# Block-window attention into a mixture of experts on one core: first products of all pair passes from scaled float16 parts

## The chip, the cores and the metric

One core of a Trainium2 chip runs the whole program. The metric is the device time of one execution in microseconds; the kernel's time is the median over runs. TensorE (PE) multiplies, VectorE (DVE), ScalarE (ACT) and GpSimd (POOL) do elementwise work and move results out of PSUM, SyncE (SP) issues all DMA transfers, in order.

## The reference

```python
# q, k, v: [4, 8, 768, 64]; block = 32, window = 16
k_sum = k.reshape(B, H, 24, 32, D).max(axis=3)
v_sum = v.reshape(B, H, 24, 32, D).mean(axis=3)
a = softmax(concat([scale * q @ k.T masked to |i - j| < 16,
                    scale * q @ k_sum.T + log(32)]))
attn = a @ concat([v, v_sum])
x = attn.transpose(0, 2, 1, 3).reshape(3072, 512)
p = domain_probs / (domain_probs.sum(-1, keepdims=True) + 1e-9)
for e in range(4):                       # w1[e]: 512 x 1024, w2[e]: 1024 x 512
    out += p[:, e:e + 1] * (np.maximum(x @ w1[e], 0) @ w2[e])
```

Every token goes through all four experts; the output is float32.

## The kernel before, in words

The 3,072 tokens are eight blocks of 384 (`TB`), two to each batch entry b. A plan (line 1183) walks through six stages: block 0 with experts 0, 1; block 1 with experts 1, 0; blocks 0 and 1 together with experts 2, 3 (the plain stages, named [0], [1] and [0,1] here); then three pairs of blocks, pair 1 (blocks 2, 3) with experts 3, 2, 1, 0, pair 2 with 0 to 3 and pair 3 with 0 to 3. The attention that makes the x of a later pair runs in between, in steps that have each a due time on the scale of the plan (`steps`, `advance`); pair 1's x is made in the plain stages, pair 2's in pair 1, pair 3's in pair 2. Nothing of it is left for pair 3. The order within each engine is then made by a scheduler from the program order and priorities, so that rows of an engine can stand otherwise than in the code.

Precision comes from parts: a matrix is split into a high and a low part, and a product is three matmuls, high x high, high x low, low x high. The plain stages use float32 parts (`ph` tiles, `plain_units`): per expert and hidden chunk of 128, twelve matmuls of 384 columns; ACT makes the high part `hh` of the relu, and DVE the low part `hl` (`to_h`), which frees the PSUM bank. The second product (`po` tiles, 128x512) sums over the chunks.

The pair stages (`pair_units`) use a scheme with seven instead of eight products for the two blocks and two halves of the weights (`SEVEN`): for each of four index pairs i, seven combinations of w1 (`WS`) times seven combinations of x (`XS`), six matmuls of 128x384 each (two chunks by three part products), in PSUM tiles pha, phb, phc, phd. The combinations of x are made by `x_operands` from raw x that was written to DRAM (`xs`, `xraw`) as attention left PSUM.

Pairs 1 and 2 have float32 parts. `w1_operands` makes the seven combinations of w1 with their parts in pair 1 (ACT copies, DVE and POOL subtractions), and stores each of the seven (256 KB) in DRAM; pair 2 loads them again, seven loads a set. Pair 3 (`SCALED`) has float16 parts in both products. For that the weights and v are scaled by powers of two found from their largest magnitudes: in pair 2, DVE scans the w1 combinations (`scan_w1`, 16 rows of 256 columns for each expert) and w2 (`scan_w2`, 8 rows of 512 columns); v's maximum is found for b = 3 alone (`setup_v_part`). `spread_maxima` writes the maximum of each partition to DRAM and loads all 128 to every partition; `take_maxima` reduces them and makes a scale and its inverse. `prepare` loads raw w1 and w2 again and makes the scaled float16 combinations of w1 (`ws`, `wss`) and parts of w2 (`w2s`) at listed points of pair 2's last expert and of pair 3 (`LATE`, `FIRST`, `SECOND`); raw x is scaled by DVE in `x_operands`. `mixed` folds the inverse scales into the mixing weights `pw` (a copy `pm`).

`with_fetch` fetches the next expert's weight sets at units 1 and 8 of a second product. In SBUF a pool tag "w1" has NW1 = 14 tiles, of which a float32 set takes 7, and a tag "x" has NX tiles, of which the x of a pair takes 14 in float32 and 7 in float16.

Everything goes through a recording helper, so nearly all instructions show line 79 in the profile; they are told apart by the names of their tiles. The names: `aw` are the attention weights, `awT` their transposes (by DMA), `px` the attention output in PSUM, `psc` the scores, `ms`, `rs`, `nb` softmax tiles, `vch` a chunk of v, `vsr` its block sums, `found` the columns of maxima and scales, `xr` raw x of a pair, `x_t`, `xl_t`, `xh_t` combinations of x.

Of the kernel before, what the change touches and what calls it, by code (L numbers as in the profile page):

```python
# [66 lines left out]
def attn_moe(ctx: ExitStack, tc: tile.TileContext, qvL, qv0, v0L, kD, kT, vT, w1L, w2L, dpL, cst, out):  # L67
# [69 lines left out]
    pending, last_matmul = [], [None]  # L137

    def spread_maxima():

        for t in pending:
            m, k, name = t["m"], t["k"], t["name"]
            room = dram.tile([P, k], F32, name=f"{name}d")
            SP.dma_start(room, m)
            t["every"] = every = sb.tile([P, P, k], F32, name=f"{name}e", tag="hs", bufs=2)
            flat = room.rearrange("p k -> (p k)").rearrange("(o n) -> o n", o=1)
            SP.dma_start(every.rearrange("p q k -> p (q k)"), flat.broadcast_to([P, P * k]))

    def take_maxima():
        while pending and "every" in pending[0]:  # L150
            t = pending.pop(0)
            ins = V.tensor_reduce(t["m"], t["every"].rearrange("p q k -> p k q"), axis=AX.X, op=ALU.max)
            behind(ins, last_matmul[0])
            t["then"](*scales(t["m"], t["k"]))

    def scales(m, k):

        both = facts(2 * k)
        s, inv = both[:, 0:k], both[:, k : 2 * k]
# [72 lines left out]

    def setup_v(b):
        for hp in range(H // 2):
            if b < SCALED or hp == H // 2 - 1:
                setup_v_part(b, hp)
        vsr, top = vstats[b]
        stack_v(b, vsr)
        if b == SCALED:
            m = facts(1)  # L240
            V.tensor_reduce(m, top, axis=AX.X, op=ALU.max)
            pending.append(dict(m=m, k=1, name="v", then=lambda *s: v_scale.update({b: s})))
# [164 lines left out]
    def to_x(n):  # L407
# [15 lines left out]
        A.mul(xs[:, 0], pair[0], 1.0 / ASC)  # L423
        A.mul(xs[:, 1], pair[1], 1.0 / ASC)
# [9 lines left out]
    def x_operands(pr):  # L434
        if pr == SCALED:
            xp = {}
            for w in XS:
                both = sb.tile([P, 2, 2, TB], F16, name=f"x{pr}_{w}", tag="x", bufs=NX)
                xp[w] = both[:, 0], both[:, 1]
        else:  # L440
            xp = {w: [x_half(f"x{v}{pr}_{w}") for v in "hl"] for w in XS}
# [341 lines left out]
    def w1_operands(e, pr):  # L783
        ws = {w: w1_part(f"w1{w}{e}_{pr}") for w in WS}
        if (e, pr) in stored:
            for w in WS:
                SP.dma_start(ws[w].bitcast(F32), stored[e, pr][w])
# [13 lines left out]
        parts("11", a11, PL)  # L801
        parts("22", a22, V)
# [3 lines left out]
        parts("s2", a11, V)  # L806
        parts("s1", a22, PL)
        parts("s3", a21, V)
        parts("12", a12, PL)
# [12 lines left out]
    KINDS = ("11", "12", "22", "s3")  # L822

    def scan_w1(ws, i, m):

        if m in SCANS:
            w = SCANS[m]
            largest(top1[:, KINDS.index(w), i : i + 1], ws[w][:, 0:256].bitcast(F32))

    SCANS = {0: "11", 1: "s3", 2: "12", 3: "22"}  # L830

    def scan_w2(fc, w):
        largest(top2[:, fc : fc + 1], w[0].bitcast(F32))

    def maxima_of(e):

        V.tensor_reduce(kinds, top1, axis=AX.X, op=ALU.max)
        V.tensor_tensor(kinds[:, 0:1], kinds[:, 0:1], kinds[:, 3:4], op=ALU.add)
        V.tensor_reduce(most[:, 0:1], kinds[:, 0:3], axis=AX.X, op=ALU.max)
        V.tensor_reduce(most[:, 1:2], top2, axis=AX.X, op=ALU.max)  # L840

        def then(s, inv):
            V.tensor_scalar_mul(s[:, 1:2], s[:, 1:2], W2TOP)
            V.tensor_scalar_mul(inv[:, 1:2], inv[:, 1:2], 1.0 / W2TOP)
            w_scale[e] = s, inv

        pending.append(dict(m=most, k=2, name=f"w{e}", then=then))
# [3 lines left out]
    def prepare():  # L851

        jobs = [
            (which, e, i)
            for e in PAIRS[-1][1]
            for which, i in ((0, 0), (0, 1), (1, 0), (1, 1), (0, 2), (0, 3), (1, 2), (1, 3))
        ]
# [2 lines left out]
        def load(which, e, i):  # L860
            raws[which, e, i] = [load_weights((w1L, w2L)[which], e, 2 * i + j, "12"[which] + "s") for j in range(2)]

        def parts(t, raw, s):
            behind(A.activation(t[:, 0], raw, AF.Copy, scale=s), last_matmul[0])
            V.scalar_tensor_tensor(t[:, 1], raw, s, t[:, 0], op0=ALU.mult, op1=ALU.subtract)
# [3 lines left out]
        for (which, e, i), after in zip(jobs, jobs[1:] + [None]):  # L869
            s = w_scale[e][0][:, which : which + 1]  # L870
            r1, r2 = raws.pop((which, e, i))
            if after:
# [1 line left out]
            if which == 1:
                w = sb.tile([P, 2, 2, 512], F16, name=f"w2s{e}_{i}", tag="w2", bufs=FC)
                for j, r in enumerate((r1, r2)):
                    parts(w[:, j], r, s)
                    half2[e, 2 * i + j] = w[:, j, 0], w[:, j, 1]
                    yield
                continue  # L880
            a11, a12 = r1[:, 0:256], r1[:, 256:512]
            a21, a22 = r2[:, 0:256], r2[:, 256:512]
            ws = ready[SCALED, e, i] = {}

            def group(names, raw):
                t = sb.tile([P, 2, 256 * len(names)], F16, name=f"ws{names[0]}{e}_{i}", tag="w1", bufs=NW1)
                parts(t, raw, s)
                for o, w in enumerate(names):
                    ws[w] = tuple(t[:, v, 256 * o : 256 * (o + 1)] for v in range(2))

            group(("11", "12"), r1)
            group(("22",), a22)
            PL.tensor_tensor(a22, a21, a22, op=ALU.add)
            PL.tensor_tensor(a21, a11, a21, op=ALU.subtract)
            yield
            group(("s3", "s1"), r2)
            PL.tensor_tensor(a11, a22, a11, op=ALU.subtract)
            PL.tensor_tensor(a12, a12, a11, op=ALU.subtract)
            yield
            group(("s2", "s4"), r1)  # L900
            yield
# [2 lines left out]
    FIRST, SECOND = (0, 2, 4, 7, 9, 11, 14, 16, 18, 20), (1, 2, 4, 5, 7, 8, 10, 11, 13, 14)
    LATE = (0, 1, 2, 4, 5, 7, 8, 13, 14, 15, 16)

    mix = {}

    def mixed(e):

# [363 lines left out]
```

## Time and profile before

| | us |
|---|---|
| median of 3 runs | 1165.96 (1163.51 to 1166.89) |
| profiled execution, time | 1165.11 |
| profiled execution, span | 1163.3 |
| PE busy | 1136.3 (98%) |
| DVE / ACT / POOL busy | 747.8 / 597.8 / 521.3 |

| stage | from, to (us) |
|---|---|
| [1], expert 1 | 132.4 to 174.8 |
| [1], expert 0 | 174.8 to 214.2 |
| [0,1], expert 2 | 214.2 to 290.8 |
| [0,1], expert 3 | 290.8 to 375.0 |
| pair 1 | 375.0 to 653.4 |
| pair 2 | 653.4 to 924.4 |
| pair 3 | 924.4 to 1163 |

The profile is of one execution. A row of a group gives engine, operation, output and input tile, shape, count, then the busy time and the mean duration in ns of one, then the idle time before such instructions and what ended it. A row of the chain gives start, duration, engine, tile and how many instructions in a run. A row of the waits reads: who waited, for whom, total us, times, longest. A row of the windows gives the stretch, its length, and the busy time (and count) of each engine, then the granted clock of PE as a share of full speed, the DMA share and GB/s.

### The profile page before, as it was taken

The page shows a single profiled execution, that of the slowest core. Times are in us where ns is not written, and L with a number is a line of the kernel's source. Part 1 is how long each engine was busy: PE and PEld are TensorE (multiplying, and loading weights), DVE is VectorE, ACT ScalarE, POOL GpSimd, SP SyncE. Part 2 cuts the span into 40 slices and gives each one's busy share as a digit, 9 for nine tenths or more (in the row PEclk, how much of TensorE's full clock was granted, in tenths as well). Part 3 has the DMA queues.
Part 4 walks back from the last instruction along what each step waited for, and adds up shares of the span by engine and source line. Part 5 has one row for each costly group of instructions (what it writes and reads, how often), then busy time and mean ns, then how long its engine had stood idle before and what let it go on. Part 6 is the DMA issues. An engine that isn't in the chain of part 4 may idle for free.

```text
span 1163.3 us, 21120 instructions
## 1 busy us (share of the span) xinstructions
PE 1136.3 (98%) x7212; PEld 921.4 (79%) x7212; DVE 747.8 (64%) x1783; ACT 597.8 (51%) x1682; POOL 521.3 (45%) x642
## 2 busy tenths in 40 slices
PE   9898899999989999999999999999999999999998
PEld 7888789998977989889898998989888754545454
DVE  5679776554797745658677665747557874646461
ACT  5578567665565746447365433525334453535350
POOL 2398687846695746548266212212102222222220
PEclk9999999999998999999999999999999999999999
DMA  6699787966986877879994677849581532222211
GB/s 241 204 286 323 232 234 238 272 176 175 328 241 177 271 229 257 253 242 301 304 269 126 193 208 206 285 124 334 136 250 54 140 98 73 74 73 73 73 37 55
DMA packets 195564, 228.78 MB, mean 197 GB/s; under 512 B 82560, under 2 KB 119296, under 8 KB 195456
## 3 DMA queue, kind: packets, MB, share of 16 engines
q1 hardware_dynamic: 195456, 227.43, 65.5%
q8 instruction: 57, 0.93, 0.3%
q14 instruction: 51, 0.42, 0.1%
HBM read 153.32 MB, written 57.15 MB: 181 GB/s over the span
## 4 chain that ended last, share of the span: by engine, by line
PE 75%; DMA 8%; DVE 6%; POOL 4%; ACT 3%; issue 2%; SPq 1%; POOLq 0%; ACTq 0%; DVEq 0%
PE po L79 38%; PE phb L79 12%; PE pha L79 7%; PE phc L79 4%; PE phd L79 4%; PE psc L79 3%; PE ph L79 3%; PE px L79 2%; DMA wr<-in_w2L 2%; DMA vch<-in_vT 1%; DMA wr<-in_w1L 1%; PE pav L79 1%; DMA awT<-aw 1%; DVE xr L79 1%; POOL wl L79 1%
## 5 line engine op out<-in xcount | busy, mean ns | idle before, releaser
L79 PE MATMUL po<-w,hh 128*128 128x512 f32 x1152 | 361.6, 395 | 0.0
L79 PEld LDWEIGHTS po<-w,hh 128*128 128x128 f32 x1152 | 212.7, 189 | 45.4
L79 PE MATMUL po<-w,hl 128*128 128x512 f32 x576 | 227.4, 397 | 0.0
L79 POOL TENSOR_TENSOR ks<-kr,ks 128x304 fp32r<-128x304 f32 x112 | 100.0, 899 | 184.7 <-ACT ks L79 176.3
L79 PEld LDWEIGHTS po<-w,hl 128*128 128x128 f32 x576 | 108.4, 188 | 23.8
L79 DVE CUSTOM_DVE_ANT_0 ms<-psc,c_sb 96x152 f32<-96x152 f32 x256 | 68.9, 306 | 80.0 <-PE psc L79 76.1
L79 PE MATMUL po<-w2s,hh 128*128 128x512 f16 (+1 forms) x400 | 114.2, 370 | 0.0
L79 ACT ACTIVATE ms<-ms,nb 96x152 f32<-96x152 f32 x256 | 104.3, 416 | 17.2 <-DVE nb L79 16.6
L79 DVE TENSOR_TENSOR aw<-ms,aw 96x512 f16<-96x512 f32 x112 | 77.9, 728 | 29.0 <-ACT aw L79 28.6
L79 POOL TENSOR_TENSOR wr1s<-wr1s 128x256 f32<-128x256 f32 x32 | 27.8, 870 | 151.3 <-DVE ws L79 136.7
L79 PE MATMUL ph<-xh,wh 128*128 128x384 f32 x256 | 88.1, 348 | 4.5 <-ACT wh L79 3.7
L79 ACT CAST ks<-kr 128x304 fp32r<-128x304 f32 x112 | 48.2, 445 | 82.6 <-PE psc L79 65.5
L79 PE MATMUL ph<-xl,wh 128*128 128x384 f32 x256 | 87.2, 341 | 2.3 <-DVE xl L79 2.3
L79 PE MATMUL ph<-xh,wl 128*128 128x384 f32 x256 | 87.4, 343 | 1.6 <-POOL wl L79 1.6
L79 ACT CAST aw<-ms 96x512 f16<-96x512 f32 x112 | 53.3, 523 | 61.9 <-issue 33.3
L79 POOL TENSOR_TENSOR wl<-wr,wh 128x512 fp32r<-128x512 f32 x44 | 63.0, 1436 | 44.4 <-ACT wh L79 44.0
L79 PE MATMUL phb<-xh_t,w1s 128*128 128x384 f32 x256 | 76.8, 340 | 1.4 <-ACT phb L79 1.3
L79 PE MATMUL pha<-xh,w 128*128 128x384 f32 x256 | 74.2, 335 | 0.0
L79 PEld LDWEIGHTS <-hh 128*128 128x128 f16 x400 | 39.1, 98 | 43.2
L79 PE MATMUL po<-w2s,hl 128*128 128x512 f16 (+1 forms) x200 | 73.0, 370 | 0.0
L79 ACT CAST v<-qv 128x256 bf16<-128x256 f32 x112 | 44.3, 405 | 54.7 <-PE px L79 39.0
L79 POOL TENSOR_TENSOR qv<-qv,v 128x256 f32<-128x256 f32 x56 | 40.7, 738 | 70.2 <-ACT v L79 69.9
(162 smaller groups left out, 2603.6 us busy)
## 6 DMA issues: line engine op xcount, KB each, us to landing
w<-wd SPq DMA_DIRECT2D x56, 512.0 KB, 5.5
wr<-in_w1L SPq DMA_DIRECT2D x76, 256.0 KB, 4.2
qv<-in_qvL SPq DMA_DIRECT2D x56, 320.0 KB, 4.3
wd<-w SPq DMA_DIRECT2D x32, 512.0 KB, 4.2
wds<-w1s SPq DMA_DIRECT2D x64, 256.0 KB, 3.0
kr<-in_kD SPq DMA_DIRECT2D x56, 256.0 KB, 3.9
w1s<-wds SPq DMA_DIRECT2D x56, 256.0 KB, 4.1
wd<-w SPq DMA_DIRECT2D x48, 256.0 KB, 3.6
```

What stands on the lines that cost most here:

```text
L79: ins = getattr(self.engine, name)(*a, **kw)
```

## The change

The first product of all three pairs is made from scaled float16 parts; the second product of pairs 1 and 2 stays in float32 parts, that of pair 3 in float16.

- `w1_operands` makes each set once, in scaled float16, in four groups (w1 parts "11" and "12" together, "22", "s3" and "s1", "s2" and "s4"), on ACT (scaled copy) and DVE (low part), and stores four tensors (256 + 128 + 256 + 256 KB). Pairs 2 and 3 load those. A set takes four "w1" tiles instead of seven. `prepare` has only w2 left.
- The maxima of w1 are sought in the plain stages with block 1, [1] and [0,1], one scan of 512 columns behind each hidden chunk's product; `with_scale` reduces and spreads them in the second product of the same expert (`spread_maximum`, `take_maximum`, now for one key at a time). w2's maxima stay in pair 2.
- v's maxima are sought for b = 1, 2, 3, each with its own round trip through DRAM, and `setup_v_part` has due times of its own for each part.
- `xs` is scaled as ACT takes it out of PSUM; the scaling of `xr` in `x_operands` goes. The x operands of all pairs are float16 and take seven "x" tiles.
- `mixed` scales `pw` in place at the start of every pair expert.
- In the last plain expert the fetches stand at units 5 and 10 instead of 1 and 8.

The diff, cut to its core:

```diff
     def setup_v_part(b, hp):
...
-        if b == SCALED:
-            V.tensor_reduce(top[:, hp : hp + 1], ch, axis=AX.X, op=ALU.max, apply_absolute_value=True)
+        V.tensor_reduce(vtop[:, hp : hp + 1], ch, axis=AX.X, op=ALU.max, apply_absolute_value=True)
...
+    def spread_maximum(key, m, room_of=("hs", 2)):
+
+        name = "m" + "_".join(str(w) for w in key)
+        room = dram.tile([P, 1], F32, name=f"{name}d")
+        SP.dma_start(room, m)
+        every = sb.tile([P, P], F32, name=f"{name}e", tag=room_of[0], bufs=room_of[1])
+        SP.dma_start(every, room.rearrange("p k -> (p k)").rearrange("(o n) -> o n", o=1).broadcast_to([P, P]))
+        chains[key] = m, every
...
-        A.mul(xs[:, 0], pair[0], 1.0 / ASC)
-        A.mul(xs[:, 1], pair[1], 1.0 / ASC)
+        for g in range(2):
+            A.activation(xs[:, g], pair[g], AF.Copy, scale=scale["px", tb // 2])
...
-            if pr == SCALED:
-                behind(V.tensor_scalar(raw, raw, v_scale[pr][0], None, op0=ALU.mult), last_matmul[0])
...
-        def parts(w, raw, lo):
-            hi, low = ws[w][:, 0:256], ws[w][:, 256:512]
-            A.copy(hi, raw)
-            lo.tensor_tensor(low, raw, hi.bitcast(F32), op=ALU.subtract)
-            stored[e, pr][w] = dram.tile([P, 512], F32, name=f"wd{w}{e}_{pr}")
-            SP.dma_start(stored[e, pr][w], ws[w].bitcast(F32))
+        def group(names, raw):
+            t = rooms[names]
+            A.activation(t[:, 0], raw, AF.Copy, scale=s)
+            V.scalar_tensor_tensor(t[:, 1], raw, s, t[:, 0], op0=ALU.mult, op1=ALU.subtract)
+            d = stored[e, i][names] = dram.tile([P, 2, 256 * len(names)], F16, name=f"wd{names[0]}{e}_{i}")
+            SP.dma_start(d, t)
...
-                if pr == SCALED - 1:
-                    scan_w1(ready[pr, e, i], n, m)
...
+    def with_scale(units, e):
+        for n, us in enumerate(units):
+            if n == 0:
+                maximum_of(("w1", e), top1)
+            if n == 4:
+                take_maximum(("w1", e), TOP)
             yield us
...
-                yield mm1(fc, tb, w1[fc], KC // 2 if fc < early else 0)
+                us = mm1(fc, tb, w1[fc], KC // 2 if fc < early else 0)
+                if tb == 1:
+                    largest(top1[:, fc : fc + 1], w1[fc][0].bitcast(F32))
+                yield us
...
-        yield from with_fetch(units) if last else units
+        if 1 in tbs:
+            units = with_scale(units, e)
+        yield from with_fetch(units, fetches=(5, 10)) if last else units
...
-        order = range(FC // 2) if small else orders[pr, e]
+        mixed(pr, e)
+        order = orders[pr, e]
...
-        steps += [(k - 2.0, setup_k, b), (k - (0.5 if b == 1 else 1.0), setup_v, b)]
+        steps.append((k - 2.0, setup_k, b))
+        first = k - (1.4 if b == 1 else 1.9)
+        for hp in range(H // 2 - 1):
+            steps.append((first + 0.3 * hp, lambda b, hp=hp: setup_v_part(b, hp), b))
+        steps += [(first + 0.9, setup_v, b), (k + 2.0, scale_of_v, b)]
```

On PE, at the start of pair 1: the last matmuls of stage [0,1]'s second product and the first ones of pair 1's first product (`pha`). Before:

```order
L79 MATMUL po_3_2_5112<-w_7_4713,hh_3_7_4707 128x512 x2
L79 MATMUL po_3_2_5112<-w_7_4713,hl_3_7_4708 128x512
L79 MATMUL pha_3_0_5266<-xh_11_4730,w_0_4773 128x384
L79 MATMUL pha_3_0_5266<-xl_11_4731,w_0_4773 128x384
L79 MATMUL pha_3_0_5266<-xh_11_4730,w_0_4773 128x384 x2
```

and after:

```order
L79 MATMUL po_3_2_5155<-w_7_4803,hh_3_7_4796 128x512 x2
L79 MATMUL po_3_2_5155<-w_7_4803,hl_3_7_4797 128x512
L79 LDWEIGHTS ws_0_5017
L79 MATMUL pha_3_0_5338<-x_11_4825,ws_0_5017 128x384
L79 LDWEIGHTS ws_0_5017
L79 MATMUL pha_3_0_5338<-x_11_4825,ws_0_5017 128x384
```

The matmuls stand in the same place with the same shapes; the float16 ones have a row for each load of weights, which the float32 ones have not.

On DVE, in expert 1 of stage [1], around the first two `hl` of its product (`wh` are its w1 parts). Before:

```order
L79 TENSOR_REDUCE vsr_1869<-vch_1_1873 128x24
L79 TENSOR_SCALAR rs_1918<-rs_1918 96x4
L79 RECIPROCAL rs_1918<-rs_1918 96x4
L79 TENSOR_TENSOR ms_1916<-ms_1916,rs_1918 96x608
L79 TENSOR_TENSOR aw_747<-ms_1916,aw_747 96x512
L79 TENSOR_REDUCE vsr_1869<-vch_2_1876 128x24
L79 TENSOR_TENSOR aw_747<-ms_1916,aw_747 96x4x48
L79 SCALAR_TENSOR_TENSOR hl_1_4_1955<-ph_1_4_1941,hh_1_4_1954 128x384
L79 SCALAR_TENSOR_TENSOR hl_1_5_1995<-ph_1_5_1981,hh_1_5_1994 128x384
```

and after:

```order
L79 TENSOR_REDUCE found<-wh_4_1440 128x1
L79 TENSOR_TENSOR ms_2029<-ms_2029,rs_2031 96x608
L79 TENSOR_REDUCE vsr_1771<-vch_3_1882 128x24
L79 TENSOR_REDUCE found<-vch_3_1882 128x1
L79 TENSOR_TENSOR aw_747<-ms_1925,aw_747 96x512
L79 TENSOR_TENSOR aw_747<-ms_1925,aw_747 96x4x48
L79 TENSOR_REDUCE found<-wh_5_1493 128x1
L79 SCALAR_TENSOR_TENSOR hl_1_4_1964<-ph_1_4_1950,hh_1_4_1963 128x384
L79 TENSOR_REDUCE found<-wh_6_1525 128x1
L79 SCALAR_TENSOR_TENSOR hl_1_5_2005<-ph_1_5_1991,hh_1_5_2004 128x384
```

Two scans of w1, a maximum of v and a second normalisation now stand ahead of the first `hl`, and a third scan ahead of the second.

On DVE, at the end of expert 3's first product in stage [0,1], around the `aw` rows that PE waits for at 346 us. Before:

```order
L79 TENSOR_TENSOR xr_0_4744<-xr_0_4744 128x192
L79 SCALAR_TENSOR_TENSOR hl_3_6_4625<-ph_3_6_4611,hh_3_6_4624 128x384
L79 TENSOR_SCALAR rs_4597<-rs_4597 96x4
L79 RECIPROCAL rs_4597<-rs_4597 96x4
L79 TENSOR_TENSOR xl_t_4739<-xr_0_4744,xh_t_4738 128x2x96
L79 TENSOR_TENSOR ms_4595<-ms_4595,rs_4597 96x608
L79 SCALAR_TENSOR_TENSOR hl_3_7_4668<-ph_3_7_4654,hh_3_7_4667 128x384
L79 TENSOR_TENSOR aw_747<-ms_4355,aw_747 96x512
L79 TENSOR_TENSOR aw_747<-ms_4355,aw_747 96x4x48
L79 SCALAR_TENSOR_TENSOR hl_3_7_4708<-ph_3_7_4694,hh_3_7_4707 128x384
L79 TENSOR_TENSOR xl_t_4741<-xr_0_4744,xh_t_4740 128x2x96
L79 TENSOR_TENSOR w1s_1_5054<-wr_2_5060,w1s_1_5054 128x256
```

and after:

```order
L79 TENSOR_TENSOR x_t_4829<-xr_0_4832,x_t_4829 128x2x96
L79 TENSOR_REDUCE found<-wh_7_4739 128x1
L79 TENSOR_TENSOR x_t_4830<-xr_0_4832,x_t_4830 128x2x96
L79 TENSOR_REDUCE found<-found 128x1
L79 TENSOR_TENSOR xr_0_4832<-xr_0_4832 128x192
L79 TENSOR_SCALAR rs_4685<-rs_4685 96x4
L79 RECIPROCAL rs_4685<-rs_4685 96x4
L79 TENSOR_TENSOR ms_4683<-ms_4683,rs_4685 96x608
L79 TENSOR_TENSOR aw_747<-ms_4440,aw_747 96x512
L79 TENSOR_TENSOR aw_747<-ms_4440,aw_747 96x4x48
L79 SCALAR_TENSOR_TENSOR hl_3_7_4797<-ph_3_7_4783,hh_3_7_4796 128x384
L79 TENSOR_REDUCE found<-mv_2e 128x1
```

Ahead of the `aw` rows there are now the last scan of w1, the maximum over its columns and two more combinations of x; the subtraction of w1's parts has gone from behind them, and the reduction of v's spread maximum, `found<-mv_2e`, stands there.

More of the change, by code (lines that the diff above doesn't have):

```diff
@@ L135, in behind, with take_maximum @@
         )
[L137 to L159, printed above, removed]
+    last_matmul, chains = [None], {}
+    def spread_maximum(key, m, room_of=("hs", 2)):
[5 more added lines that the diff above has]
+        chains[key] = m, every
+    def take_maximum(key, top):
+        m, every = chains.pop(key)
+        behind(V.tensor_reduce(m, every, axis=AX.X, op=ALU.max), last_matmul[0])
+        both = facts(2)
+        s, inv = both[:, 0:1], both[:, 1:2]
         V.tensor_scalar(m, m, LEAST, MOST, op0=ALU.max, op1=ALU.min)
@@ L224, in setup_v_part @@
             vsr = sb.tile([P, G, NB], F32, name=f"vsr{b}", tag="vsr")
-            vstats[b] = vsr, facts(G) if b == SCALED else None
-        vsr, top = vstats[b]
+            vstats[b] = vsr
+        vsr = vstats[b]
         ch = chunk(f"vch{b}_{hp}")
@@ L229, in setup_v_part, with scale_of_v @@
         block_stats(ch, vsr, hp, ALU.add)
-        if b == SCALED:
-            V.tensor_reduce(top[:, hp : hp + 1], ch, axis=AX.X, op=ALU.max, apply_absolute_value=True)
+        V.tensor_reduce(vtop[:, hp : hp + 1], ch, axis=AX.X, op=ALU.max, apply_absolute_value=True)
     def setup_v(b):
[L234 to L242, printed above, removed]
+        setup_v_part(b, H // 2 - 1)
+        stack_v(b, vstats.pop(b))
+        m = facts(1)
+        V.tensor_reduce(m, vtop, axis=AX.X, op=ALU.max)
+        spread_maximum(("v", b), m, ("hs", 2) if b < SCALED else ("x", NX))
+    def scale_of_v(b):
+        take_maximum(("v", b), TOP)
+        s = facts(1)
+        V.tensor_scalar_mul(s, scale["v", b][0], 1.0 / ASC)
+        scale["px", b] = s
     def stack_v(b, vsr):
@@ L434, in x_operands @@
     def x_operands(pr):
-        if pr == SCALED:
[L436 to L441, printed above, removed]
+        xp = {}
+        for w in XS:
+            both = sb.tile([P, 2, 2, TB], F16, name=f"x{pr}_{w}", tag="x", bufs=NX)
+            xp[w] = both[:, 0], both[:, 1]
         def split(w, raw, c, lo):
@@ L781, in attn_moe, with w1_operands @@
     WS = ("11", "s2", "s1", "s3", "12", "s4", "22")
[L783 to L787, printed above, removed]
-            return ws
-        r1, r2 = (load_weights(w1L, e, 2 * pr + j, "1") for j in range(2))
+    def w1_operands(e, i):
+        rooms = {
+            names: sb.tile([P, 2, 256 * len(names)], F16, name=f"ws{names[0]}{e}_{i}", tag="w1", bufs=NW1)
+            for names in (("11", "12"), ("22",), ("s3", "s1"), ("s2", "s4"))
+        }
+        ws = {
+            w: tuple(t[:, v, 256 * o : 256 * (o + 1)] for v in range(2))
+            for names, t in rooms.items() for o, w in enumerate(names)
+        }
+        if (e, i) in stored:
+            for names, t in rooms.items():
+                SP.dma_start(t, stored[e, i][names])
+            return ws
+        s = scale["w1", e][0]
+        r1, r2 = (load_weights(w1L, e, 2 * i + j, "1") for j in range(2))
         a11, a12 = r1[:, 0:256], r1[:, 256:512]
         a21, a22 = r2[:, 0:256], r2[:, 256:512]
-        stored[e, pr] = {}
-        def parts(w, raw, lo):
-            hi, low = ws[w][:, 0:256], ws[w][:, 256:512]
-            A.copy(hi, raw)
-            lo.tensor_tensor(low, raw, hi.bitcast(F32), op=ALU.subtract)
-            stored[e, pr][w] = dram.tile([P, 512], F32, name=f"wd{w}{e}_{pr}")
-            SP.dma_start(stored[e, pr][w], ws[w].bitcast(F32))
-        parts("11", a11, PL)
-        parts("22", a22, V)
+        stored[e, i] = {}
+        def group(names, raw):
[4 more added lines that the diff above has]
+            SP.dma_start(d, t)
+        group(("11", "12"), r1)
+        group(("22",), a22)
         PL.tensor_tensor(a22, a21, a22, op=ALU.add)
@@ L805, in w1_operands @@
         PL.tensor_tensor(a11, a22, a11, op=ALU.subtract)
[L806 to L809, printed above, removed]
+        group(("s3", "s1"), r2)
         PL.tensor_tensor(a12, a12, a11, op=ALU.subtract)
-        parts("s4", a12, V)
+        group(("s2", "s4"), r1)
         return ws
     PAIRS = ((1, (3, 2, 1, 0)), (2, (0, 1, 2, 3)), (3, (0, 1, 2, 3)))
-    top1 = facts(2 * FC).rearrange("p (w i) -> p w i", i=FC // 2)
-    top2, kinds, most = facts(FC), facts(4), facts(2)
+    top1, top2 = facts(FC), facts(FC)
     def largest(room, part):
@@ L820, in largest, with maximum_of @@
         behind(ins, last_matmul[0])
[L822 to L847, printed above, removed]
+    def maximum_of(key, top):
+        m = facts(1)
+        V.tensor_reduce(m, top, axis=AX.X, op=ALU.max)
+        spread_maximum(key, m)
@@ L849, in attn_moe @@
     half2 = {}
     def prepare():
[L853 to L857, printed above, removed]
-        raws = {}
[L860 to L865, printed above, removed]
+        jobs = [(e, i) for e in PAIRS[-1][1] for i in range(FC // 2)]
@@ L867, in prepare, with load @@
+        raws = {}
+        def load(e, i):
+            raws[e, i] = [load_weights(w2L, e, 2 * i + j, "2s") for j in range(2)]
         load(*jobs[0])
         yield
-        for (which, e, i), after in zip(jobs, jobs[1:] + [None]):
-            s = w_scale[e][0][:, which : which + 1]
-            r1, r2 = raws.pop((which, e, i))
+        for (e, i), after in zip(jobs, jobs[1:] + [None]):
+            s = scale["w2", e][0]
+            rs = raws.pop((e, i))
             if after:
                 load(*after)
[L874 to L901, printed above, removed]
@@ L903, in attn_moe @@
-    preparing = prepare()
[L904 to L909, printed above, removed]
-        gts = range(2 * SCALED * (TB // P), 2 * (SCALED + 1) * (TB // P))
-        if not mix:
-            t = sb.tile([P, len(gts) + 1, E], F32, name="pm", tag="ksr")
-            for k, gt in enumerate(gts):
-                mix[gt] = t[:, k]
-            mix["all"] = t
-        t, back = mix["all"][:, : len(gts), e : e + 1], mix["all"][:, len(gts), e : e + 1]
-        inv = w_scale[e][1]
-        V.tensor_tensor(back, v_scale[SCALED][1], inv[:, 0:1], op=ALU.mult)
-        V.tensor_scalar(
-            t, pw[:, gts[0] : gts[-1] + 1, e : e + 1], back, inv[:, 1:2], op0=ALU.mult, op1=ALU.mult
-        )
+            w = sb.tile([P, 2, 2, 512], F16, name=f"w2s{e}_{i}", tag="w2", bufs=FC)
@@ new lines, in prepare, with mixed @@
+            for j, r in enumerate(rs):
+                behind(A.activation(w[:, j, 0], r, AF.Copy, scale=s), last_matmul[0])
+                V.scalar_tensor_tensor(w[:, j, 1], r, s, w[:, j, 0], op0=ALU.mult, op1=ALU.subtract)
+                half2[e, 2 * i + j] = w[:, j, 0], w[:, j, 1]
+                yield
+    preparing = prepare()
+    FIRST, SECOND, LATE = (3, 9, 15, 21), (2, 5, 8, 11), (8, 13, 14, 15, 16)
+    def mixed(pr, e):
+        gts = slice(2 * pr * (TB // P), 2 * (pr + 1) * (TB // P))
+        p = pw[:, gts, e : e + 1]
+        V.tensor_scalar(p, p, scale["v", pr][1], scale["w1", e][1], op0=ALU.mult, op1=ALU.mult)
+        if pr == SCALED:
+            V.tensor_scalar(p, p, scale["w2", e][1], None, op0=ALU.mult)
@@ L941, in mm2_halves @@
         gt = tb * (TB // P) + t
-        pe = (mix[gt] if gt in mix else pw[:, gt])[:, e : e + 1]
+        pe = pw[:, gt, e : e + 1]
         for c in range(2):
@@ L969, in mm2 @@
             gt = tb * (TB // P) + t
-            pe = (mix[gt] if gt in mix else pw[:, gt])[:, e : e + 1]
+            pe = pw[:, gt, e : e + 1]
             added[gt] = added.get(gt, 0) + 1
@@ L985, in attn_moe @@
     before = None
-    for pr, es in PAIRS[:-1]:
+    for pr, es in PAIRS:
         for e in es:
@@ L1044, in mm1 @@
                 PE.matmul(ph, whi[:, c, :], xl, start=False, stop=False)
-                PE.matmul(ph, wlo[:, c, :], xh, start=False, stop=c == KC - 1)
+                last_matmul[0] = PE.matmul(ph, wlo[:, c, :], xh, start=False, stop=c == KC - 1)
             if c1 == KC:
@@ L1097, in pair_units @@
                 o = new(k) if first else bank[k]
-                both = ready[pr, e, i][w]
-                both = both if small else [both[:, v * 256 : (v + 1) * 256] for v in range(2)]
-                wh, wl = (v.rearrange("p (c f) -> p c f", f=P) for v in both)
+                wh, wl = (v.rearrange("p (c f) -> p c f", f=P) for v in ready[pr, e, i][w])
                 xh, xl = xp[x]
```

32 lines of the change are left out of this document (13 added, 19 removed).

## The prediction

> **What bounds the kernel now.** I read the page first, then the chain, then the waits of PE, then windows by stage. Busy time and clock of the page:
> ```profile
> span 1163.3 us, 21120 instructions
> PE 1136.3 (98%) x7212; PEld 921.4 (79%) x7212; DVE 747.8 (64%) x1783; ACT 597.8 (51%) x1682; POOL 521.3 (45%) x642
> PEclk9999999999998999999999999999999999999999
> ```
> PE is busy for 98% of the span and no other engine for more than 64%. The one slice that shows an 8 in the clock is the thirteenth, at 349 to 378 us. The windows say which stages have slack on DVE and which have none; 290.6 to 375 is expert 3 of stage [0,1], 132 to 175 is expert 1 of stage [1], 653.4 to 723 an expert of pair 2, 924.4 to 951 the start of pair 3.
> ```profile
> core 0: us, PE busy (x) PEld busy (x) DVE busy (x) ACT busy (x) POOL busy (x), PEclk, DMA share, GB/s
> 132.00:175.00 43.00, 40.65 (x259) 36.55 (x259) 32.33 (x80) 28.39 (x87) 32.48 (x36) 0.96 0.86 257
> 290.60:329.00 38.40, 38.40 (x295) 37.67 (x294) 30.39 (x63) 21.99 (x64) 27.59 (x31) 1.00 0.95 303
> 329.00:346.60 17.60, 15.76 (x114) 12.33 (x113) 17.31 (x39) 13.98 (x49) 17.00 (x21) 1.00 0.89 261
> 348.70:355.30 6.60, 4.71 (x35) 4.00 (x35) 5.09 (x13) 4.46 (x15) 4.21 (x7) 0.50 1.01 281
> 653.40:723.00 69.60, 69.60 (x451) 62.59 (x450) 41.74 (x111) 30.06 (x89) 17.02 (x24) 1.00 0.78 214
> 924.40:951.00 26.60, 24.87 (x152) 14.78 (x152) 21.08 (x43) 15.38 (x31) 6.46 (x8) 1.00 0.54 144
> ```
> In the pair stage PE is busy for all 69.60 us with DVE at 41.74: there the time is the sum of the matmuls and nothing else. In expert 1 of stage [1], and from 329 us on in stage [0,1], DVE has 10.7 us and 0.3 us left. PE's waits, longest groups, over the whole span:
> ```profile
> PE px L79 <- DMA awT<-aw: 8.1, 4, 4.7
> PE ph L79 <- ACT wh L79: 3.7, 4, 1.2
> PE phb L79 <- ACT phb L79: 2.6, 3, 1.3
> PE ph L79 <- DVE xl L79: 2.3, 1, 2.3
> ```
> The longest wait, 4.7 us, is named for a DMA. The timeline of DVE and of PE at its place shows that the transfer itself had waited for DVE:
> ```profile
> 344.49 1.22 DVE L79 TENSOR_TENSOR aw<-ms,aw 96x512 f16<-96x512 f32 x1
> 346.30 0.34 DVE L79 TENSOR_TENSOR aw<-ms,aw 96x192 f16<-96x192 f32 x1
> 350.60 0.61 PE L79 MATMUL px<-awT,v 128*64 128x96 f16 x10 [4.65 <-DMA awT<-aw]
> ```
> The last aw row ends at 346.64, the transpose lands 4 us later, and DVE was busy for 17.31 of the 17.60 us before. So this wait is DVE's, and its second price is the clock of 0.50 in the 6.6 us after it: 3.3 us of work lost. The Trainium skill, TensorE: Matmul & The Clock Gate, "HAM oscillation — how this bites in real kernels", says that a gap of PE over some 3.4 us brings the slow clock; the 4.65 us gap with 0.50 behind it agrees.
>
> **Term 1, the first product in float16.** Per expert of a pair the first product has 4 x 7 x 6 = 168 matmuls of 384 columns; two pairs of four experts have 1,344. The chain lists runs of twelve of them, in pairs 1 and 2 (float32) and in pair 3 (float16), and one of six at the end of pair 2's first products:
> ```profile
> 389.09 2.08 PE pha L79 x12
> 658.06 2.08 PE pha L79 x12
> 884.75 1.04 PE phb L79 x6
> 943.25 1.95 PE pha L79 x12
> ```
> Float32 takes 2.08/12 = 173.3 ns from start to start, float16 1.95/12 = 162.5. The change is 10.8 ns x 1,344 = 14.5 us, with 1.1 us of rounding in the two rows. Since PE is full in these stages (69.60 of 69.60), all of it reaches the end. What goes from DVE, ACT, POOL and DMA in the pair stages (subtractions, scans, 256 KB loads) had been hidden under that full PE and is worth nothing by itself.
>
> **Term 2, the start of pair 3.** Before, the scaled weights and the scaling of x crowd DVE there (21.08 of 26.60 us), and PE waits; its waits from 924 us on begin:
> ```profile
> PE phb L79 <- ACT phb L79: 1.3, 1, 1.3
> PE phb L79 <- DVE phc L79: 0.5, 1, 0.5
> ```
> After, pair 3's w1 sets are loads and x comes scaled, so both should go: -1.8, bounds -1.8 and 0. Nothing is late next: a set's loads are issued at least one set of 42 matmuls (6.8 us) ahead, and the loads of stored parts took 4 to 5.5 us from issue to landing (page):
> ```profile
> w<-wd SPq DMA_DIRECT2D x56, 512.0 KB, 5.5
> w1s<-wds SPq DMA_DIRECT2D x56, 256.0 KB, 4.1
> ```
>
> **Term 3, changes of type on PE.** Pairs 1 and 2 now go from float16 first products to float32 scores and second products and back. Two places show such changes:
> ```profile
> 376.93 0.34 PE L79 MATMUL phd<-xh_t,w1s 128*128 128x384 f32 x1
> 377.20 0.40 PE L79 MATMUL px<-awT,v 128*64 128x96 f16 x10
> 924.21 0.40 PE L79 MATMUL po<-w,hl 128*128 128x512 f32 x1
> 924.45 0.66 PE L79 MATMUL pha<-x,ws 128*128 128x384 f16 x3
> ```
> From a float32 first product to px it is 270 ns, some 95 over the usual 173; from the float32 second product to pha it is 240, nothing beyond a matmul of 512 columns. The second is the nearest to what is added, so I take +0.6; if each of some 70 new changes cost 95 ns, it would be 6.6. Downwards, about 28 px groups that now follow float16 could save those 95 ns, 2.7; I take -0.3.
>
> **Term 4, DVE in expert 1 of stage [1].** Added there are 8 scans of w1 and 4 maxima of v, beside a maximum over all partitions and small steps for the scale. Their nearest rows:
> ```profile
> L79 DVE TENSOR_REDUCE found<-w 128x1 f32<-128x512 f32 x32 | 21.5, 677 | 10.4 <-PE po L79 10.4
> L79 DVE TENSOR_REDUCE found<-vch 128x1 f32<-128x768 f32 x4 | 3.8, 942 | 0.0
> L79 DVE TENSOR_REDUCE found<-ve 128x1 f32<-128x128 f32 x1 | 0.3, 276 | 0.0
> L79 DVE TENSOR_SCALAR found<-found 128x1 f32<-128x1 f32 x11 | 1.5, 146 | 0.0
> L79 DVE TENSOR_TENSOR w1s<-wr,w1s 128x256 fp32r<-128x256 f32 x48 | 27.8, 588 | 7.9 <-ACT w1s L79 7.8
> ```
> 8 x 0.677 + 4 x 0.942 = 9.2, and a chain of 0.28 + 5 x 0.146 = 1.0: 10.2 us against the 10.7 that DVE has free. In the order, two scans, a maximum of v and a normalisation stand ahead of the first two hl rows, which free the banks that PE fills. By 10.2 of 10.7 almost nothing reaches PE on the mean; the rows come bunched, so I take +2, bounds 0 and +8 (most of it reaches PE).
>
> **Term 5, DVE in expert 3 of stage [0,1].** Again 8 scans (5.4) and 4 maxima of v (3.8), and two chains (2.0); of the subtractions of w1's parts, some 5 (0.588 each) move behind the aw rows: about +8.3 ahead of the same aw rows. The window 290.6 to 329 has 38.40 - 30.39 = 8.0 us free, 329 to 346.6 has 0.3. Were the free time usable in full, nothing would reach PE; since part of it lies in waits for data, I take half, +4; bounds 0 and +8.3, and 3.3 more if a second window falls to half clock.
>
> **Sum**, against the profiled execution's 1165.1 (its span 1163.3 and 1.8 around it): 1165.1 - 14.5 - 1.8 + 0.6 - 0.3 + 2 + 4 = 1155.1. The median of the runs shown is 0.85 above the profiled one, so 1156.
>
> **Rivals.** (a) All of the gain: the free time of DVE takes the new rows in. For it: 10.2 fits in 10.7 and 8.3 nearly in 8.0. Against: the stall at 346 exists with less on DVE. It gives 1165.1 - 14.5 - 1.8 = 1148.8, down to 1146 with the saving at px; should the new order put aw earlier, so that the stall and its slow clock go, 5 to 8 less.
>
> (b) DVE eats most of it: terms 4 and 5 come near their bounds, +6 and +8: 1163. The waits would stand in the same two stages.
>
> (c) Slower: DVE bounds both of those experts and sets the clock off. Rows of 10.2 and 8.3 on DVE reach PE in full, each with a wait over 4 us and 3.3 us of half clock behind it: 18.5 + 6.6 = 25, so 1165.1 - 16.3 + 25 = 1174. It decides from 20 us lost (16.3 + 3.5). For it: 348.7 to 355.3 shows that one wait does this. Against: the free time that the windows show.
>
> (d) Also slower: the 173.3 is no price of float32 but of the place, of the weights and pieces that stream in beside pairs 1 and 2 (DMA share 0.78 in the row of 653.4, 0.54 at the start of pair 3). Float16 would then keep 173.3 and term 1 is nothing: 1165.1 - 1.8 + 0.3 + 6 = 1170. Against it stands the row of 884.75: six float32 matmuls in 1.04, 173.3 again, in a stretch where nothing moves:
> ```profile
> 884.00:886.00 2.00, 2.00 (x20) 1.74 (x18) 1.60 (x6) 0.16 (x1) 0.00 (x0) 1.00 0.00 0
> ```
> The DMA share there is 0.00, so this rival is nearly ruled out. By the Trainium skill, TensorE: Matmul & The Clock Gate, "Back-to-back issue gap", the gap is N/2.4 + 2.5 ns, 162.5 for 384 columns, and no type enters, by which the change would gain nothing in term 1; the float16 rows agree with its figure and the float32 rows, at 173.3, do not.
>
> (e) The chains of maxima hold SP: 11 round trips instead of 5, each a store and a load that waits for it.
> ```profile
> w3d<-found SPq DMA_DIRECT2D x1, 1.0 KB, 3.1
> w3e<-w3d SPq DMA_DIRECT2D x1, 128.0 KB, 5.5
> ```
> Behind a waiting load on SP are queued the loads of weights and the transposes of aw. SP stands still for about 3.1 us each time; six more would cost 18 if all reached PE, and the one that lies near aw at 346 alone about 3. It is in the upper bound of term 5.
>
> **Chances.** Forecast (1152.5 to 1159): 0.47. (a): 0.28. (b), which lies on both sides of the bound below: 0.15. (c) with (e): 0.07. (d): 0.03. A measurement of this kernel tells about 0.3%, 3.5 us, from no change. Faster: 0.47 + 0.28 + 0.08 = 0.83; same: 0.07 of (b) and 0.01 of (c) = 0.08; slower: 0.09. Range: from 1146, the end of (a) without the vanished stall, to 1163, the end of (b); outside stay (c), (d) and the vanished stall.
>
> **What would show it.** Right: runs of twelve first products in pairs 1 and 2 at 1.95; the experts of pairs 1 and 2 shorter by 1.8 us each (14.5/8); no waits for phb and phc at pair 3's start; scans and maxima of v among DVE's rows at 132 to 175 and 290 to 346, with DVE near full and PE waiting there for hl, xl or aw by some 6 us more. Wrong: first products at 2.08; stages [1] and [0,1] unchanged or shorter; or a second stretch with clock 0.50, or waits of PE for w sets in the pair stages, where I expect none.

## The result, and the profile after

The changed kernel took 1224.22 us (median of 4, 1221.05 to 1225.6) beside 1166.03 of the kernel before: a ratio of 1.0499, interval 1.0472 to 1.0526. It is 58 us slower, where 10 us less was forecast. The profiled execution took 1225.22. Its page:

```profile
span 1223.1 us, 20542 instructions
PE 1138.7 (93%) x7212; PEld 828.7 (68%) x7212; DVE 701.1 (57%) x1724; ACT 563.9 (46%) x1570; POOL 427.4 (35%) x530
PEclk9999998899988999999989999998998999999999
```

PE is idle for 1223.1 - 1138.7 = 84.4 us, before for 27.0: 57.4 more. Busy it is for 2.4 us more, though term 1 alone takes 14.5 off; so, by estimate, some 17 us have come to the matmuls from a slow clock, which the third row shows in seven slices instead of one. Every other engine has less to do than before. This is a kernel that waits, not one with more work. The lengths of the stages, from the starts of the first matmuls:

| stage | before | after | difference |
|---|---|---|---|
| [1], expert 1 | 42.4 | 48.8 | +6.4 |
| [1], expert 0 | 39.4 | 56.5 | +17.1 |
| [0,1], expert 2 | 76.6 | 80.6 | +4.0 |
| [0,1], expert 3 | 84.2 | 96.8 | +12.6 |
| pair 1 | 278.4 | 287.8 | +9.4 |
| pair 2 | 271.1 | 282.2 | +11.1 |
| pair 3 | 238.9 | 236.9 | -2.0 |

The windows of these stages after (columns as before the change); the first is expert 1 of stage [1], then expert 0, then expert 3 of [0,1], pair 1 and pair 2:

```profile
133.40:182.20 48.80, 42.56 (x252) 36.90 (x253) 31.88 (x88) 27.36 (x82) 30.62 (x33) 0.93 0.68 156
182.20:238.70 56.50, 44.35 (x299) 38.69 (x298) 29.33 (x87) 27.01 (x80) 27.24 (x30) 0.89 0.76 221
319.30:416.10 96.80, 80.58 (x533) 71.44 (x532) 75.00 (x185) 51.24 (x154) 54.63 (x66) 0.91 0.64 189
416.10:703.90 287.80, 270.75 (x1757) 193.62 (x1756) 188.12 (x438) 156.26 (x434) 129.96 (x167) 0.98 0.67 200
703.90:986.10 282.20, 266.56 (x1682) 190.44 (x1682) 142.75 (x364) 108.20 (x314) 54.36 (x78) 0.98 0.56 147
```

No engine is full in any of them: DVE has 27 of 56.5 us free in the worst, and the DMA share is lower than before (0.76 against 0.82 there). PE's waits, longest groups:

```profile
PE px L79 <- DMA awT<-aw: 25.4, 7, 8.4
PE psc L79 <- DVE nb L79: 12.0, 3, 11.0
PE psc L79 <- POOL qs L79: 11.6, 5, 6.4
PE phb L79 <- ACT phb L79: 9.9, 3, 8.2
PE pha L79 <- DVE hl L79: 6.6, 1, 6.6
```

The five rows name four different releasers, so a name alone explains nothing; each has to be followed. The longest one, 8.4 us, stands in expert 3 of [0,1]. SP's timeline there (start, duration of the issue, transfer):

```profile
348.49 0.33 SPq L79 DMA_DIRECT2D mv_2d<-found  x1
356.10 0.33 SPq L79 DMA_DIRECT2D mv_2e<-mv_2d  x1
356.53 0.37 SPq L79 DMA_DIRECT2D xr<-xd  x1
357.00 1.33 SPq L79 DMA_TRANSPOSE awT<-aw  x1
```

The stretch from 349 to 357 us as a window:

```profile
349.00:357.00 8.00, 5.69 (x67) 5.28 (x61) 5.15 (x10) 1.93 (x6) 2.67 (x3) 1.00 0.01 1
```

And the wait of PE in its timeline:

```profile
363.14 0.61 PE L79 MATMUL px<-awT,v 128*64 128x96 f16 x10 [8.45 <-DMA awT<-aw]
```

SP issues the store of v's maxima (`mv_2d`, 512 bytes) and then the load of them to all partitions (`mv_2e`), which must wait until the store has landed. For 7.6 us SP issues nothing, and in the window the DMA engines move 1 GB/s at a share of 0.01: SP is not held by traffic. The transpose of aw, which PE needs, stands two places behind. The wait for qs is the same thing one step longer: SP held from 215.74 to 223.11, the piece of q and v behind it late, ACT and POOL late, PE late. SP's timeline:

```profile
215.74 0.49 SPq L79 DMA_DIRECT2D mw_0d<-found  x1
223.11 0.33 SPq L79 DMA_DIRECT2D mw_0e<-mw_0d  x1
223.53 0.39 SPq L79 DMA_DIRECT2D qv<-in_qvL  x1
```

Then ACT's row, with its wait of 9.03 us:

```profile
230.17 0.40 ACT L79 CAST v<-qv 128x256 bf16<-128x256 f32 x1 [9.03 <-DMA qv<-in_qvL]
```

Then PE's:

```profile
236.02 0.92 PE L79 MATMUL psc<-ks,qs 128*96 128x152 f32 x4 [6.38 <-POOL qs L79]
```

A trip holds DVE as well, which works in order: three times it stands before the reduction of a spread maximum, for 6.2, 8.5 and 9.6 us, ending at 163.84, 185.49 and 299.08. The second of these:

```profile
185.49 0.29 DVE L79 TENSOR_REDUCE found<-mw_1e 128x1 f32<-128x128 f32 x1 [8.46 <-DMA mw_1e<-mw_1d]
```

The three waits of 11.0, 8.2 and 6.6 us are in pairs 1 and 2 and have one shape: ACT, POOL and DVE wait one for the other for raw x, and behind such a row stands what PE needs. For the wait of 8.2 us SP issues the store and the load of raw x around 840 us. SP:

```profile
839.46 0.56 SPq L79 DMA_DIRECT2D xd<-xs  x1
845.28 0.32 SPq L79 DMA_DIRECT2D xr<-xd  x1
```

ACT:

```profile
848.21 0.60 ACT L79 CAST x<-xr 128x192 f16<-128x192 f32 x2 [8.12 <-DMA xr<-xd]
```

DVE:

```profile
849.22 1.08 DVE L79 TENSOR_TENSOR xr<-xr 128x192 f32<-128x192 f32 x2 [7.90 <-POOL x L79]
```

PE:

```profile
850.84 1.44 PE L79 MATMUL phb<-x_t,wss 128*128 128x384 f16 x4 [8.22 <-ACT phb L79]
```

The copy of `phb` that PE waits for here stands behind ACT's own row of x; in the other two cases `nb` and `hl` stand behind DVE's `xr` rows. The wait of 8.2 us is in the first product of pair 2's last expert but one. In the order of DVE's rows before the change, the first `xr` row of pair 3 stood in the first product of pair 2's last expert, between its last two `hl` rows; after, it stands ahead of the first `hl` of the last expert but one, one and a half experts earlier than the code emits it. Before, the 14 tiles of a pair's float32 x filled the pool "x", so the next pair's could not start until the old ones were free. Two float16 sets of 7 fit together, the scheduler moves the next pair's rows up, and ACT and DVE, which work in order, then stand for a transfer. That the free tiles are what let the rows move is read from the code and the order; no run changed the number of tiles.

So two theories. **T**: the round trips of the maxima hold SP for 7 to 9 us each, and what is queued behind them comes late. **X**: DVE (in the case shown, ACT) stands before rows of the next pair's x. The rival **D** is the prediction's (c): the added scans and maxima fill DVE in the plain stages.

### The profile page after: what moved, and what is told of

It reads as the page before. It is cut to its first block, busy times and chain, and to the rows that moved or that the text cites. A ratio compares the mean times of both kernels' runs of the same rounds, so it can differ in the third digit from the quotient of the medians.

```text
span 1223.1 us, 20542 instructions
## 1 busy us (share of the span) xinstructions
PE 1138.7 (93%) x7212; PEld 828.7 (68%) x7212; DVE 701.1 (57%) x1724; ACT 563.9 (46%) x1570; POOL 427.4 (35%) x530
## 5 line engine op out<-in xcount | busy, mean ns | idle before, releaser
L79 PE MATMUL po<-w,hh 128*128 128x512 f32 x1152 | 367.6, 400 | 1.5 <-DVE acc L79 1.5
L79 PEld LDWEIGHTS <-wss 128*128 128x128 f16 x1152 | 111.2, 99 | 88.4 <-issue 17.9
L79 PEld LDWEIGHTS <-ws 128*128 128x128 f16 x864 | 83.6, 99 | 64.8 <-issue 12.6
L79 PE MATMUL phb<-x_t,wss 128*128 128x384 f16 x576 | 112.5, 332 | 12.7 <-ACT phb L79 9.9
L79 PE MATMUL pha<-x,ws 128*128 128x384 f16 x576 | 110.6, 332 | 6.6 <-DVE hl L79 6.6
L79 DVE SCALAR_TENSOR_TENSOR acc<-po,pw,acc 128x512 f32<-128x512 f32 (+1 forms) x73 | 52.2, 737 | 70.6 <-PE po L79 70.6
L79 PE MATMUL psc<-ks,qs 128*96 128x152 f32 x448 | 61.3, 261 | 24.3 <-DVE nb L79 12.0
L79 PEld LDWEIGHTS psc<-ks,qs 128*96 128x96 f32 x448 | 53.7, 167 | 35.2 <-POOL qs L79 13.4
```

The costliest lines, as they stand in the source:

```text
L79: ins = getattr(self.engine, name)(*a, **kw)
```

## Experiments

**Trips away, x late, both.** `e1_const` replaces the scales by constants (so it computes no scales of its own):

```diff
-        SP.dma_start(room, m)
...
-        SP.dma_start(every, ...broadcast_to([P, P]))
...
+        PL.memset(s, top / k)
+        PL.memset(inv, k / top)
```

> Scales of v, w1 and w2 are constants (the powers of two that the inputs give), so none of the 11 round trips through DRAM is made; all scans and maxima stay on DVE. Theory T (the trips hold SP and DVE in the plain stages, where the profile after is 41 us longer than before): most of the 41 us goes, 1224 - 38 = 1186, and the stretches at 161, 189, 236, 363 us lose their waits for awT and qs. Theory X (DVE stands before rows of the next pair's x operands, 35 us in pairs 1 and 2): those stay. Rival D (the scans and maxima themselves fill DVE): no change, 1220 to 1224.

Measured: 1164.87 (median of 8; ratio to before 0.9996, 0.9976 to 1.0016). 59 us went, more than T's 38: with the trips the x stalls have shrunk to 2.4 us and less, though the x rows stand as early as in the changed kernel. D has fallen, since all scans are still there.

`e2_xlate` puts the first copies of each x part behind the latest matmul:

```diff
+            copied = A.copy(hi, raw)
+            if w in ("11", "22"):
+                behind(copied, last_matmul[0])
```

> The first copies of each part of the next pair's x operands wait for the latest matmul in program order, so that they stand in the last expert's second product again; all else as in the changed kernel. Theory X: the waits of 11.0, 8.2 and 6.6 us in pairs 1 and 2 and the slow clock behind them go, 1224 - 35 = 1189. Theory T alone: no change, 1220 to 1226. Rival D: no change.

Measured: 1203.5 (2 runs, ratio 1.0327, 1.0295 to 1.0359): 20.7 off, not 35. The three waits are gone, but a new one of 5.5 us, for `hl`, has come in pair 1.

`e3_both` has both edits.

> Constant scales without round trips, and the x operands late; scans and maxima stay on DVE. T and X together: the gain of the first product is left, 1166 - 16 = 1150, with 0 to 6 us lost to DVE in the plain stages. Rival D: at least the 41 us of the plain stages stay, 1190.

Measured: 1160.81 (10 runs, ratio 0.9965, 0.9951 to 0.9978). Only 4 better than `e1_const`, and 11 short of the expectation; 5 of these are in expert 0 of stage [0] (52.4 us, 47.8 in the changed kernel), where the three kernels with constants are all slower. That was not followed up.

`e6_pe_xlate` spreads the maxima on chip; one transpose of a column that is repeated 128 times puts all maxima on every partition:

```diff
+        PL.tensor_copy(wide, m.broadcast_to([P, P]))
+        every = ps_av.tile([P, 512], F32, name=f"{name}e", tag="av")[:, 0:P]
+        behind(PE.transpose(every, wide, ident), last_matmul[0])
+        V.tensor_reduce(m, every, axis=AX.X, op=ALU.max)
```

> x operands late, and the maxima spread without DMA: POOL copies the column of maxima to 128 columns, PE transposes it into PSUM, DVE reduces from there; scales are computed as in the changed kernel. T and X: as e3_both, plus 11 small copies, transposes and chains on PE, POOL and DVE, 1150 to 1155. If the chain on DVE itself (not the DMA) were the cost: 1180 or more.

Measured: 1154.35 (4 runs, ratio 0.9895, 0.987 to 0.9919), as expected, with all scans, maxima and scales in it. PE's longest groups of waits there:

```profile
PE ph L79 <- ACT wh L79: 4.9, 3, 2.6
PE phb L79 <- ACT phb L79: 4.1, 1, 4.1
PE px L79 <- DMA awT<-aw: 3.5, 4, 2.2
```

The wait for awT has come down from 25.4 us to 3.5, those for nb and hl over 5 us are gone.

**Trips alone, in the kernel before.** Six round trips that nothing uses; each ends in a reduction on DVE, as in the changed kernel:

```diff
+            if n == 0:
+                trip_out(("w", e))
+            if n == 4:
+                trip_in(("w", e))
```

> The kernel before, with six dummy round trips of 0.5 KB and 64 KB added in the plain stages where the changed kernel has its own (two for v, four for w1); nothing uses their result. Theory T (the trip holds SP, 7 to 9 us each, with loads and transposes behind it): the plain stages grow by 25 to 40 us, 1166 + 32 = 1198, with waits of PE for awT and qs. Rival (the added DVE rows, or the new place of the w1 sets, make the plain stages longer): 1166 to 1170.

Measured: 1205.42 (2 runs, ratio 1.033, 1.030 to 1.036): 39 us more, with the products and scans of the kernel before. The trip in expert 1 of stage [1]:

```profile
172.26 0.33 SPq L79 DMA_DIRECT2D mw_1d<-found  x1
173.06 0.33 SPq L79 DMA_DIRECT2D qv<-in_qvL  x1
...
175.47 1.62 SPq L79 DMA_TRANSPOSE awT<-aw  x1
182.25 0.33 SPq L79 DMA_DIRECT2D mw_1e<-mw_1d  x1
183.36 0.60 SPq L79 DMA_DIRECT2D xd<-xs  x1
```

The stages [1] expert 1, [0,1] expert 2 and expert 3 grew by 10.9, 7.9 and 16.4 us, the experts of the pairs by 0.5 at most. That is 35.2 us in the stages with trips, 5.9 for each trip; another 5.8 of the profile's 42.1 lie ahead of stage [1], before the first trip at 136.34, and are not a trip's. This is the cost of a whole trip: DVE stands for it here too, 12.4 us before the reduction at 297.44, and what SP's part is and what DVE's is not told apart.

**Eight bytes a row instead of four.** The maxima in two columns:

```diff
-        room = dram.tile([P, 1], F32, name=f"{name}d")
+        room = dram.tile([P, 2], F32, name=f"{name}d")
```

> The changed kernel, with each maximum in two columns, so that a store has 8 bytes for each partition (1.0 KB, 128 KB for the load) as the merged stores of the kernel before had. In the traces stores of 1.0 KB landed in 3.1 to 5.3 us, those of 0.5 KB in 7.1 to 9.9. If the 4-byte rows are what makes the store slow, SP is held 4 to 5 us instead of 8 and about half of the loss goes: 1185 to 1200. If the load on the queues makes it slow: 1220 to 1226.

Measured: 1187.51 (2 runs, ratio 1.0176, 1.0152 to 1.0201), 37 us off with twice the bytes moved. The landing times (the last column, us from issue) in the changed kernel:

```profile
mw_1d<-found SPq DMA_DIRECT2D x2, 0.5 KB, 8.5
mw_0d<-found SPq DMA_DIRECT2D x2, 0.5 KB, 8.3
mv_2d<-found SPq DMA_DIRECT2D x1, 0.5 KB, 7.6
```

and with two columns:

```profile
mw_1d<-found SPq DMA_DIRECT2D x2, 1.0 KB, 5.7
mw_0d<-found SPq DMA_DIRECT2D x2, 1.0 KB, 3.9
mv_2d<-found SPq DMA_DIRECT2D x1, 1.0 KB, 2.8
```

**The x order without trips.**

`e5_pe` is `e6_pe_xlate` without the edit to the x parts.

> Maxima spread by PE instead of DMA, the x operands where the changed kernel has them (early). If the stalls at x need the trips (the trip delays the store and load of raw x, for which DVE then stands): e6_pe_xlate plus 4 to 8 us, 1154 + 6 = 1160. If they are independent of the trips: e6_pe_xlate plus 21, as between the changed kernel and e2_xlate: 1175.

Measured: 1159.33 (2 runs, ratio 0.9935, 0.9911 to 0.9959): 5.0 above `e6_pe_xlate`. With it the two causes make a square:

| | x early | x late | x early costs |
|---|---|---|---|
| trips by DMA | 1224.2 | 1203.5 | 20.7 |
| spread by PE | 1159.3 | 1154.4 | 5.0 |
| the trips cost | 64.9 | 49.1 | |

The intervals of the two kernels without trips just overlap, so the 5.0 is uncertain; that it is far below 20.7 is not. The early x rows are dear mainly because a trip has just made SP late with raw x: the three stalls lie 7 to 13 us behind the trips whose loads SP issued at 619.75, 832.81 and 909.28.

**The scans.** `e3_both` without the scans of w1 and the maxima of v:

```diff
-                    largest(top1[:, fc : fc + 1], w1[fc][0].bitcast(F32))
...
-        V.tensor_reduce(vtop[:, hp : hp + 1], ch, axis=AX.X, op=ALU.max, apply_absolute_value=True)
```

> As e3_both, and the scans of w1 and the maxima of v in the plain stages left out as well (scales are constants). The cost of these rows on DVE that reaches PE is the difference to e3_both (1160.8): terms 4 and 5 of the prediction have 2 + 4 = 6 us: 1155. If DVE takes them in: 1161.

Measured: 1159.83 (5 runs, ratio 0.9943, 0.9916 to 0.9969), 1.0 below `e3_both`, which is within the intervals; by the two ratios it is 2.6. In the profiles the stages from [1], expert 1, to [0,1], expert 3, take 246.6 us together with the rows and 246.8 without them. DVE takes the rows in.

**The load further back.** The stores as they were, the load behind a later matmul:

```diff
+        behind(SP.dma_start(every, flat), last_matmul[0])
```

> The changed kernel with the same stores of 0.5 KB and the same loads, but each load is put behind a later matmul and so stands 2 to 31 rows behind its store in SP's order instead of 1 or 2 (the scale is taken later as well). If it is SP standing before the load that costs, most holds shrink where the load has moved and much of the 58 us goes: 1165 to 1195. If the transfers themselves or the late scale cost: 1215 to 1230.

Measured: 1198.1 (2 runs, ratio 1.0274, 1.0198 to 1.035), 26 off, 3 us above the range expected. (The first fetches of pair 1 stand at units 8 and 11 in this run, behind the later scale.) Where the load moved, SP is free between the two; but the transposes of aw take its time instead:

```profile
169.70 0.38 SPq L79 DMA_DIRECT2D mw_1d<-found  x1
...
174.60 7.99 SPq L79 DMA_TRANSPOSE awT<-aw  x1
182.69 0.52 SPq L79 DMA_DIRECT2D mw_1e<-mw_1d  x1
```

A transpose usually takes SP 1.3 us here; this one took 8.0, its first microseconds with the small store under way. So SP's stand before the load seems to be only a part of what a trip costs; the parts were not measured one by one.

**Earlier w1 sets.** `e6_pe_xlate` with the scale of w1 and the first fetches earlier:

```diff
-            if n == 4:
+            if n == 2:
                 take_maximum(("w1", e), TOP)
...
-        yield from with_fetch(units, fetches=(5, 10)) if last else units
+        yield from with_fetch(units, fetches=(3, 8)) if last else units
```

> As e6_pe_xlate, with w1's scale taken two units earlier and the first w1 sets of pair 1 fetched at units 3 and 8 of the last plain expert instead of 5 and 10. If the wait of 4.1 us for the copy of phb at pair 1's start comes from sets made late: 1154 - 4 = 1150. If not: 1154.

Measured: 1151.15 (4 runs, ratio 0.9879, 0.9814 to 0.9943). The wait of 4.1 us at pair 1's start is gone (the longest there is 2.3, for phc). Its interval overlaps that of `e6_pe_xlate`, so the further 3 us are not shown. Either of the two is faster than both kernels.

## Why the prediction was wrong, point by point

**Term 1 held.** Twelve first products of the changed kernel take 1.95 us, as the chain shows:

```profile
944.70 1.95 PE phb L79 x12
```

In `e6_pe_xlate` the seven experts of pairs 1 and 2 behind the first take 465.7 us, before 480.7: 2.1 less each, 1.8 was forecast. Rival (d) is out.

**Term 2 held**: pair 3 is 2.0 us shorter, and its waits for phb and phc are gone.

**Term 3 held** at the two kinds of change that were read: nothing is lost there. From the second product to pha it is 240 ns as before, and in the other direction five float16 matmuls and two of float32 take 733.96 - 732.69 = 1.27 us, which is 5 x 0.1625 + 2 x 0.232 = 1.28 (three float32 ones of 512 columns take 0.69 to 0.70). PE's timeline at pair 1's end:

```profile
703.67 0.40 PE L79 MATMUL po<-w,hl 128*128 128x512 f32 x1
703.91 0.99 PE L79 MATMUL pha<-x,ws 128*128 128x384 f16 x5
```

and the other direction:

```profile
732.69 0.98 PE L79 MATMUL phb<-x_t,ws 128*128 128x384 f16 x5
733.37 0.76 PE L79 MATMUL po<-w,hh 128*128 128x512 f32 x2
733.96 0.39 PE L79 MATMUL po<-w,hl 128*128 128x512 f32 x1
```

**Terms 4 and 5 failed in kind.** I took DVE's added rows for the cost of the plain stages, +2 and +4. The scans and maxima cost nothing that the runs can tell from zero (1.0 us, `e4_noscan`). The stages grew by 40 us, from a thing that I had put into the upper bound of term 5.

**The step that failed is rival (e).** "SP stands still for about 3.1 us each time; six more would cost 18 if all reached PE, and the one that lies near aw at 346 alone about 3." The price came from the one store of 1.0 KB that I quoted, the fastest of four. The trips of the change store 0.5 KB, 4 bytes a partition, and the trace of before had such a store, v's, with another time:

```profile
w0d<-found SPq DMA_DIRECT2D x1, 1.0 KB, 5.3
vd<-found SPq DMA_DIRECT2D x1, 0.5 KB, 9.9
```

9.9 us, the nearest row in size and form, would have made it 11 x 9.9 = 109 us of held SP as the upper bound, 82 more than the 27 that the five stores of before take together, where I had put 18 more. In the changed kernel the eleven stores took 6.9 to 9.1 us each. And I counted the late transfer at one place only, though I had named what is queued behind: all loads of q, v, k and weights and all transposes pass through SP. By `e8_before_trips` a trip costs 5.9 us in the plain stages. The whole of the loss there is of that kind: with the maxima spread by PE and nothing else changed (`e5_pe`) the four stages take 242.5 us together, 242.6 before the change and 282.7 after it. Each of the nine waits of PE over 3 us behind the start is also followed by a stretch at half clock, as the prediction read of the stall at 346. There are eleven such stretches where there were three before; some stand behind shorter waits, the one from 263.5 to 267.5 us behind a wait of 2.6.

**A step that was missing.** "I expect none" was said of waits in the pair stages for w sets, and that held; of x the prediction says only that it comes scaled. It does not ask what keeps the next pair's x rows in their place. That they have moved up stands in the order of DVE's rows, and the float16 tiles, which no longer fill the pool, are the likely reason: the price is about 5 us alone and 21 beside the trips.

With both away the kernel takes 1154.4, and 1156 had been forecast: the terms on PE were right, and what was added beside them was not priced. That the two times lie so near is in part luck: the 6 us of terms 4 and 5 did not come, while the profile of `e6_pe_xlate` has 3.9 us more than before ahead of stage [1] and 4.3 more in the first expert of pair 1, behind the wait of 4.1.

## What to carry to other kernels

Price a small DMA that something waits for by the row of the same size and form, not by the fastest of its kind, and ask at each place what is queued behind the waiting issue on the engine that issues all transfers, and which engine stands for the result. When an edit makes tiles smaller or fewer, ask which wait for a free tile had been keeping work in its place, and look in the order for rows that have moved up ahead of work that PE needs. A few values that every partition needs are spread without DRAM by one transpose of a repeated column: 0.3 us on PE and 0.3 to 0.5 on POOL, instead of 12 us and more over DMA.

## What the runs showed of the hardware

A store of 128 rows of 4 bytes to DRAM lands 6.9 to 10.9 us after its issue in the traces read (6.9 to 9.1, median 8.2, in the changed kernel), one of 128 rows of 8 bytes at the same places of the program after 2.7 to 6.3, median 4.1 (`e7_two_col`); in one case the DMA engines were nearly idle meanwhile (share 0.01 in the window above). What in the 4-byte rows is slow was not tried. The Trainium skill, DMA: Bandwidth & Descriptors, "Anatomy of one DMA — SWDGE (gpsimd) path", gives a nearly constant 2.0 us for setup and completion on the path of another engine; on SP's here no small store came as low, and the row width changed it by a factor of two.

Transposes by DMA that SP issued behind such a store or its load took SP 4 to 8 us instead of 1.3 in several places of the changed kernel and of `e9_load_later`. But others there took 1.3 (at 357.00 in the changed kernel, right behind a load), and some were as slow with no such transfer under way: 4.75 us at 196.21 in the changed kernel, 3.83 at 587.76 in the kernel before. So the trips are not shown to be the cause; why was not tried.
